# Batch 0 put in another order, and one load of batch 2 put later, in an attention and MLP kernel

## The chip, the core and the metric

The kernel runs on one core of one Trainium2 chip. The metric is the device time of one execution in microseconds (us): the median of several runs. A profiled execution also leaves a trace, with every instruction of the engines TensorE (PE for matmuls, PEld for the loads of their stationary operand), VectorE (DVE), ScalarE (ACT) and GpSimd (POOL), and the DMA transfers. SyncE (SP) only issues DMAs here.

## The reference, cut to what matters

Eight batches of eight heads; each head has 512 local and 32 global tokens of 64 numbers. Global queries attend to all keys; local queries attend to the global keys and to local keys at a distance of at most 32. The result, 4352 rows of 512 numbers, goes through an MLP with 2048 hidden units and the activation h * sigmoid(1.702 h).

```python
s_g = scale * np.matmul(q_g, k_all.transpose(0, 1, 3, 2))
out_g = np.matmul(sm(s_g), v_all)
s_ll = np.where(np.abs(pos[:, None] - pos[None, :]) <= window, s_ll, -1000000000.0)
a_l = sm(np.concatenate([s_lg, s_ll], axis=-1))
out_l = np.matmul(a_l, np.concatenate([v_g, v_l], axis=2))
...
h = x @ w_in
g = h * (1.0 / (1.0 + np.exp(-1.702 * h)))
return (g @ w_out)
```

## The kernel before

**Units of work.** Four heads of one batch make a quad; a batch has two, and the code calls the quad at hand `a` and the other `c`. Batch 0 is special: its quads are of class `Quad`, those of all other batches of class `Wide`. All work of a quad is a set of small methods, and the order in which the kernel calls them is the order on each engine: the schedule is written out by hand, and each engine works through its own instructions in that order.

**The methods of a `Quad`.** `Tk` and `Tq` transpose k and q on DVE (L306, L310); `ext` copies parts of the global queries beside them (L323 on ACT, L325 on DVE). `B(rnd)` writes the mask as a bias into the PSUM banks with a matmul against the identity (L335), `S(rnd)` adds the scores (L352), `X(rnd)` takes the exp on ACT (L380 for four single banks, L385 for two pairs). Each quad has two rounds, rnd 0 and 1, of two key chunks each. `gg` (through `gk`, L371) gives the scores of the global queries with the global keys, `K` those of the local queries with the global keys, and `XK` their exp (`ek`, L416). `ekU(unit)` and `U(unit)` sum weights (unit 0) and weighted values (units 1 and 2) into one bank per unit (L426, L438). `R` turns the sums into reciprocals in three DVE steps (L462, L464, L466), and `XL(h)` multiplies them in and gives one 128-row chunk of the MLP's input `xL` (L471): quad `a` gives chunks 0 and 1, quad `c` chunks 2 and 3. `eg` (DVE, L397), `Gm` (PE, L456) and `G` (DVE) make the outputs of the global queries. `zero(n, ...)` issues n filler matmuls of zeros (L646).

**PSUM.** `pbank` hands out four single banks in turn (tag "p"), for `ov`, `kb`, `og`, `hp` and `op`; `spair` gives the four others, as two pairs, for the scores and for the first four h tiles. A matmul into a bank waits until the bank's last reader is done. Within a quad of batch 0, round 1 uses the banks of round 0 again, except in quad `a`, whose round 1 has four single banks (`split=True`).

**The MLP.** `h_mm(i, fc, bank, kcs)` multiplies the chunks kcs of xL with w_in into an h tile (L586); `h_act` is a tanh on ACT (L593) and a multiplication on DVE (L594) that gives `gT`; `o_mm` multiplies with w_out (L611) and `o_out` scales and stores. The first four h tiles of batch 0 take chunks 0 and 1 first, then 2 and 3, and share their tanh in pairs (`tanh2`, L722; `act4`, L637). While the output matmuls of batch i run, the scores of batch i + 1 are put between them (`osteps` for batch 0, `phase_o` for the rest); in the h tiles of batch 1, `a.S(0)` of batch 2 follows h tile 10.

**Loads.** All loads of q, k, v and the weights cast from float32 to bfloat16 and are issued by POOL (`load`, L81; `load_v2`, L241; w_in, L254; w_out, L244), in the order of the program, among POOL's own computation: the affine select that makes `step` (L152), from which DVE makes `ident`, `band` and `bias` (L195 to L197), then constants and masks. A POOL load waits until the one eight places before it has landed. Only k of batch 0's first quad and the global rows of batch 0 come in float32 over ACT and SP, and ACT casts that k in two halves (`cast_k`, L649). w_in comes in four parts: the first two hold chunks 0 and 1, then 2 and 3, for the first eight h tiles.

```python
    warm = consts.tile([128, 512], BF16)
...
    for _ in range(7):
        nc.tensor.matmul(wp, lhsT=warm[:, :128], rhs=warm, start=True, stop=True)
```

Of the kernel before, what the change touches and what calls it, by code (L numbers as in the profile page):

```python
# [12 lines left out]
F32 = mybir.dt.float32  # L13
# [7 lines left out]
def kernel(  # L21
# [12 lines left out]
    nc = tc.nc  # L34
# [10 lines left out]
    NQ = B * 2  # L45
# [11 lines left out]
    consts = ctx.enter_context(tc.tile_pool(name="consts", bufs=1))  # L57
# [16 lines left out]
    def load(b, us=(0, 1), names="qk"):  # L74
        if b not in loaded:
            loaded[b] = (ld.tile([128, 2, 16 * D], BF16, name="rk"),
                         ld.tile([128, 2, 16 * D], BF16, name="rq"))
        s = slice(us[0], us[-1] + 1)
        for name in names:
            dst, src = ((loaded[b][0], kf), (loaded[b][1], qf))[name == "q"]  # L80
            nc.gpsimd.dma_start(out=dst[:, s], in_=src[b][:, s])  # L81
# [52 lines left out]
    def cast_g32(name, t):  # L134
        nc.vector.tensor_copy(t[:, 0:2, :D], g32[name])
# [5 lines left out]
    halves = (slice(0, 8 * D), slice(8 * D, 16 * D))  # L141
    load_g32("q", qgf)
    for f, eng in zip(halves, (nc.scalar, nc.sync)):
# [5 lines left out]
    nc.vector.memset(warm, 0.0)  # L149
    step = consts.tile([128, 289], BF16)  # L150
    nc.vector.memset(step, 1.0)
    nc.gpsimd.affine_select(  # L152
        out=step, in_=step, pattern=[[1, 289]], compare_op=ALU.is_ge,
        fill=0.0, base=-97, channel_multiplier=-1,
# [26 lines left out]
    for i in range(4):  # L181
        qt = consts.tile([128, 24, 32], F32, name="q%d" % i)
        nc.vector.memset(qt[:, 0:4, :], 0.0)
        nc.vector.memset(qt[:, 20:24, :], 0.0)
        qtiles.append(qt)

    WIN = ((0, 10), (6, 12), (14, 12), (22, 10))
    mask = consts.tile([128, 2, MW], BF16)
# [33 lines left out]
        nc.gpsimd.memset(mask_at(0, 248, 16, 12)[96:128, :, 0:4], 0.0)  # L222
        nc.gpsimd.memset(mask_at(1, 236, 16, 12)[96:128, :, 8:12], 0.0)

    load(0, (1,), "kq")
    load_turned(nc.gpsimd, rvg[:, 0:2, :D], vgf[:, 0:2])

    qgT = consts.tile([128, NQ, 40], F32)
    nc.vector.memset(qgT[:, :, 32:], 0.0)
    kgT = consts.tile([128, NQ, 32], F32)  # L230
    def transpose_g(lo, hi, names="qk"):
        for name, dst, s in (("q", qgT, rqg), ("k", kgT, rkg)):
# [15 lines left out]
    def load_rest():  # L248
        load_v2(0)
        set_consts()  # L250
        half = d_ff // 2
        for part in range(2):
            for u in range(2):
                nc.gpsimd.dma_start(out=w_in_sb[:, part, 2 * u : 2 * u + 2, :],  # L254
                                    in_=w_in_r[u][:, :, part * half : (part + 1) * half])
        load_w_out(1)
        load_w_out(0)
        mask_rest()
        for part in MASKS:
            make_mask(part)  # L260
        load(1, (0,))
        load_g(2, 4)
        load(1, (1,))
        load_vg(1)
        load_w_out(2)
        load_w_out(3)
        load(2, (0,))
        load_v(1)
        load_g(4, 8)

# [10 lines left out]
    def bank(pair, j):  # L281
        return pair[j // 2][:, j % 2, :]
# [301 lines left out]
    def h_mm(i, fc, hp, kcs):  # L584
        for kc in kcs:
            nc.tensor.matmul(hp[:, : width(i)], lhsT=w_in_c[:, fc // 8, kc, fc % 8 // 2, :, fc % 2],  # L586
                             rhs=(xL[i] if i < B else xG)[:, kc, :],
                             start=(kc == 0), stop=(kc == NKC - 1))
# [53 lines left out]
    a, c = Quad(0), Quad(1)  # L642

    def zero(n, ps, m=128, w=512):
        for _ in range(n):
            nc.tensor.matmul(ps[:m, :w], lhsT=warm[:, :m], rhs=warm[:, :w], start=False, stop=False, skip_group_check=True)  # L646

    def cast_k(f):
        nc.scalar.activation(rk[:, 0, f], k32[:, f], AF.Copy)  # L649

    cast_k(halves[0])
    cast_g32("q", rqg)
    transpose_g(0, 2, "q")
    a.ext((0, 1), True)
    cast_k(halves[1])
    a.Tk(0, 8)
    a.Tq(0, 8)
    a.Tk(8, 16)
# [4 lines left out]
    load_rest()  # L663
    a.B(0)
    a.B(1, split=True)
    zero(34, a.bk[1][3], 32, 32)
    a.S(0, added=True, part=0)
    a.S(0, added=True, part=1)
    a.X(0)
    a.S(1, split=True, added=True)  # L670
    zero(3, a.bk[1][3])
    a.X(1)
    c.Tk()
    c.ext()
# [5 lines left out]
    c.gg()  # L680
    c.X(0)
    a.eg()
    a.ekU(0)
    a.U(0)
    a.R()
    c.K()
    c.XK()
    a.ekU(1)
    a.U(1)
    a.XL(0)  # L690
    c.B(1, js=(0, 1))
    c.B(1, js=(2, 3))
    c.S(1, added=True)
    c.X(1)
    a.ekU(2)
    a.U(2)
    a.XL(1)
    a.Gm()
    gTs[0] = moe.tile([128, FC, TB], BF16, name="gT")
    pt = pts[0] = spair()  # L700
    c.ekU(0)
# [3 lines left out]
    c.U(1)  # L705
    c.ekU(2)
    c.U(2)
    c.eg()
    for fc in range(4):
        h_mm(0, fc, bank(pt, fc), (0, 1))  # L710
    c.XL(0)
    c.XL(1)
    for kc in (2, 3):
        for fc in range(4):
            h_mm(0, fc, bank(pt, fc), (kc,))
# [21 lines left out]
    nq = {b: (Wide(2 * b), Wide(2 * b + 1)) for b in (1, 2)}  # L737
    a, c = nq[1]
# [11 lines left out]
    a.S(1)  # L750
    a.X(1)
    spread_vg(1)
    nq[2][0].Tq()
    a.M(1)
    nq[2][0].Tk()
    osteps(0, (1, 2), (2, 2))
# [17 lines left out]
    a.G()  # L774
    transpose_g(4, 6)
    nq[2][0].ext(nc.gpsimd)
    load(2, (1,))
    load_v(2)
    load(3)
    osteps(0, (3, 2), (3, 3))  # L780
    a, c = nq[2]
# [4 lines left out]
    for fc in range(FC):  # L786
        if fc < 2:
            h_act(1, fc, hps[fc])
        else:
            h_step(1, fc)  # L790
        if fc == 1:
            nq[1][1].G()
        if fc == 10:
            a.S(0)
            a.X(0)
            a.M(0, nc.gpsimd)
            load_v(3)
            load(4)
            load_g(8, NQ)
# [101 lines left out]
```

## Time and profile before

| What | Value |
|---|---|
| Time, median of 3 runs | 299.2 us (299.19 to 299.46) |
| Time of the profiled execution | 299.52 us |
| Its span in the trace | 297.7 us |
| PE busy with matmuls | 291.9 us, 98% |
| VectorE, ScalarE, GpSimd busy | 219.1, 165.0, 79.7 us |
| First matmul, first matmul of the MLP | 1.26 us, 18.00 us |
| TensorE clock granted over the span | 1.00 |

The span reaches from the first to the last instruction of the trace; the time has 1.82 us more around it. All starts below are counted from the start of the span. In a row of the timeline come start and busy time, engine, line, operation, output and inputs with their shapes and the count of merged instructions; in brackets stands how long the engine had been idle before, and what ended that. Ends of matmuls are modelled: the distance between two starts tells more than their durations.

### The profile page before, as it was taken

What the parts mean: (1) busy time and instruction counts of PE and PEld (TensorE: products, weight loads), DVE (VectorE), ACT (ScalarE), POOL (GpSimd) and SP (SyncE); (2) the same over time, 40 slices, a digit from 0 to 9 for tenths busy, and PEclk for the clock granted to TensorE, in tenths of its full rate; (3) what the DMA queues carried; (4) which work ended last, traced back from release to release, by engine and by line L of the source; (5) the groups of instructions that cost most, each with busy time, mean ns of one, the idle gap of its engine ahead of it and who ended that gap; (6) DMA issues with size and microseconds to landing.
All of it is one profiled execution on the core that took longest, in us unless ns stands there. A gap on an engine that the chain in (4) does not pass through costs nothing.

```text
span 297.7 us, 8197 instructions
## 1 busy us (share of the span) xinstructions
PE 291.9 (98%) x3444; PEld 149.5 (50%) x3444; DVE 219.1 (74%) x440; ACT 165.0 (55%) x251; POOL 79.7 (27%) x130
## 2 busy tenths in 40 slices
PE   8999999999999999999999999999999999999995
PEld 5544446445454455445454455445554455446654
DVE  6669988869867887788878887778877866683320
ACT  3827375585557745567456655666446651663421
POOL 8962730589563002700072003500000000000000
PEclk9999999999999999999999999999999999999999
DMA  7999997699999213981299014901120022101122
GB/s 157 168 206 211 204 186 105 120 142 153 167 197 184 47 37 66 140 134 29 47 99 192 12 41 84 112 0 39 36 70 4 2 46 65 35 2 35 35 64 79
DMA packets 58228, 27.93 MB, mean 94 GB/s; under 512 B 47312, under 2 KB 47824, under 8 KB 58192
## 3 DMA queue, kind: packets, MB, share of 16 engines
q0 software_dynamic: 50784, 17.83, 53.2%
q1 hardware_dynamic: 7264, 9.31, 12.2%
q8 instruction: 27, 0.44, 0.6%
q10 hardware_dynamic: 144, 0.26, 0.3%
q14 instruction: 9, 0.07, 0.1%
HBM read 36.31 MB, written 8.91 MB: 152 GB/s over the span
## 4 chain that ended last, share of the span: by engine, by line
PE 96%; ACT 1%; DVE 1%; issue 0%
PE op L611 39%; PE hp L586 38%; PE s L531 6%; PE ov L557 5%; PE op L623 1%; PE w L178 1%; PE s L335 1%; PE og L568 1%; PE ov L438 1%; PE s L586 1%; ACT e L380 1%; ACT e L385 1%; DVE xL L471 0%; PE ov L426 0%; PE s L352 0%; PE s L557 0%
## 5 line engine op out<-in xcount | busy, mean ns | idle before, releaser
L611 PE MATMUL op<-w_out_sb,gT 128*128 128x512 bf16 x528 | 121.7, 379 | 0.0
L594 DVE SCALAR_TENSOR_TENSOR gT<-th,hp 128x512 bf16<-128x512 f32 (+1 forms) x140 | 91.2, 657 | 40.6 <-ACT th L593 39.7
L586 PE MATMUL hp<-xL,w_in_sb 128*128 128x512 bf16 x496 | 108.7, 379 | 0.0
L593 ACT ACTIVATE th<-hp 128x512 f32<-128x512 f32 (+1 forms) x140 | 79.8, 573 | 42.8 <-PE hp L586 40.9
L586 PEld LDWEIGHTS <-w_in_sb 128*128 128x128 bf16 x576 | 56.0, 98 | 64.9 <-DMA w_in_sb<-in_moe_w_in_dram 0.8
L611 PEld LDWEIGHTS <-gT 128*128 128x128 bf16 x528 | 49.3, 98 | 54.9
L542 ACT ACTIVATE e<-s 128x1016 bf16<-128x1016 f32 (+1 forms) x56 | 53.3, 1004 | 7.4 <-PE s L531 7.1
L626 ACT ACTIVATE ob<-op 128x512 f32<-128x512 f32 x32 | 18.9, 599 | 62.9 <-PE op L611 62.9
L97 POOL DMA_DIRECT2D v<-in_v_l_dram x35 | 28.4, 815 | 83.5 <-PE og L568 81.9
L547 DVE TENSOR_TENSOR e<-e,mask 128x1712 bf16<-128x1712 bf16 (+1 forms) x27 | 28.3, 1049 | 3.3 <-ACT e L542 3.3
L462 DVE STREAM_TRANSPOSE sT<-ov 128x512 f32<-128x512 f32 x15 | 10.7, 716 | 14.7 <-PE ov L557 12.6
L471 DVE TENSOR_TENSOR xL<-ov,rs 128x512 bf16<-128x512 f32 x30 | 19.4, 686 | 1.9 <-PE ov L438 0.5
L531 PE MATMUL s<-q,kT 32*128 32x160 bf16 (+3 forms) x672 | 19.2, 243 | 0.0
L531 PEld LDWEIGHTS <-kT 32*128 32x128 bf16 x672 | 13.1, 94 | 12.0 <-issue 6.5
L505 DVE STREAM_TRANSPOSE kT<-rk 128x512 f32<-128x512 f32 x14 | 14.5, 1033 | 0.0
L99 POOL DMA_DIRECT2D v<-in_v_g_dram x24 | 14.3, 595 | 0.0
L310 DVE STREAM_TRANSPOSE q<-rq 128x512 f32<-128x512 f32 (+1 forms) x17 | 11.5, 675 | 0.9 <-DMA rq<-in_q_l_dram 0.9
L466 DVE STREAM_TRANSPOSE rs<-rT 128x512 f32<-128x512 f32 x16 | 11.4, 711 | 0.6
L557 PE MATMUL ov<-e,v 128*32 128x128 bf16 (+3 forms) x624 | 11.7, 223 | 0.0
L557 PEld LDWEIGHTS <-v 128*32 128x32 bf16 x672 | 10.5, 97 | 0.0
L586 PE MATMUL hp<-xG,w_in_sb 128*128 128x256 bf16 x64 | 9.6, 273 | 0.0
L557 PE MATMUL ov<-e,ones 128*32 128x128 bf16 (+3 forms) x312 | 7.1, 225 | 0.0
(102 smaller groups left out, 156.3 us busy)
## 6 DMA issues: line engine op xcount, KB each, us to landing
out_dram<-ob SPq DMA_DIRECT2D x128, 64.0 KB, 1.7
v<-in_v_l_dram POOLq DMA_DIRECT2D x28, 96.0 KB, 4.4
rq<-in_q_l_dram POOLq DMA_DIRECT2D x5, 512.0 KB, 7.2
rk<-in_k_l_dram POOLq DMA_DIRECT2D x5, 512.0 KB, 9.3
w_in_sb<-in_moe_w_in_dram POOLq DMA_DIRECT2D x4, 512.0 KB, 10.5
w_out_sb<-in_moe_w_out_dram POOLq DMA_DIRECT2D x4, 512.0 KB, 12.0
v<-in_v_l_dram POOLq DMA_DIRECT2D x11, 128.0 KB, 4.7
rk<-in_k_l_dram POOLq DMA_DIRECT2D x5, 256.0 KB, 9.9
```

The lines of the kernel that those rows point to most:

```text
L97: nc.gpsimd.dma_start(out=vt[0:n, :, c, :D], in_=vs[FIRST[c] : FIRST[c] + n])
L471: nc.vector.tensor_mul(self.x[:, 2 * self.u + h, :], self.st[1 + h], self.st["rs"])
L505: nc.vector.transpose(flat[:, 0:Sl].rearrange("p (r t) -> p t r", t=16), loaded[self.b][0][:, self.u].bitcast(F32))
L531: nc.tensor.matmul(bank(self.ps, j)[:, at : at + n], lhsT=self.k[p, KEYS[c] : KEYS[c] + 128, e], rhs=self.q[p, lo:hi, r0 : r0 + nr, e], st ...
L542: nc.scalar.activation(self.E[rnd][:, 2 * i : 2 * i + 2, :n], self.ps[i][:, :, :n], AF.Exp, scale=scale)
L547: eng.tensor_mul(e, e, mask[:, rnd : rnd + 1, :n].to_broadcast([128, 4, n]))
L557: nc.tensor.matmul(ov[32 * j : 32 * j + 32, :].rearrange("p (t r) -> p t r", t=16)[:, t0:t1, r0 : r0 + nr], lhsT=lv, rhs=self.E[rnd][:, j, ...
L586: nc.tensor.matmul(hp[:, : width(i)], lhsT=w_in_c[:, fc // 8, kc, fc % 8 // 2, :, fc % 2], rhs=(xL[i] if i < B else xG)[:, kc, :], start=( ...
L593: nc.scalar.activation(th[:, :n], hp[:, :n], AF.Tanh, scale=0.851)
L594: nc.vector.scalar_tensor_tensor(gTs[i][:, fc, :n], in0=th[:, :n], scalar=1.0, in1=hp[:, :n], op0=ALU.add, op1=ALU.mult)
L611: nc.tensor.matmul(op, lhsT=gTs[i][:, fc, tci * 128 : tci * 128 + 128], rhs=w_out_sb[:, fc, :], start=(first and fc == 4 * f4), stop=(fc = ...
L626: nc.scalar.activation(ob, op, AF.Copy, scale=0.5)
```

## The change

The diff has seven parts. (1) The load of k of batch 0's second quad is issued by POOL ahead of the affine select instead of behind it; its q stays behind. The memset of `qgT` goes ahead of `ident` on DVE. (2) `cast_k` of the second half goes ahead of the first `ext` on ACT. (3) The 34 small fillers become 6 ahead of the first part of `a.S(0)`, 14 between its two parts, and 14 behind the three large fillers. (4) `c.K` goes ahead of `a.ekU(0)`, and `c.B(1)`, `c.S(1)` and `c.X(1)` go ahead of `a.U(1)` and `a.XL(0)`, with the two halves of `c.B(1)` around `a.ekU(1)`. (5) `a.Gm` goes behind the first eight matmuls of the MLP. (6) `c.eg` goes behind `c.XL(1)`. (7) q of batch 2's first quad is loaded ahead of batch 1's h tiles, with the second quad's q and k, instead of in `load_rest`; its `Tq` moves from the masks of batch 1 to behind h tile 6 of batch 1. No instruction that computes is added or taken away; the fillers stay 37 in all.

```diff
@@ -149,6 +149,7 @@
     nc.vector.memset(warm, 0.0)
     step = consts.tile([128, 289], BF16)
     nc.vector.memset(step, 1.0)
+    load(0, (1,), "k")
     nc.gpsimd.affine_select(
         out=step, in_=step, pattern=[[1, 289]], compare_op=ALU.is_ge,
         fill=0.0, base=-97, channel_multiplier=-1,
@@ -184,6 +185,9 @@
         nc.vector.memset(qt[:, 20:24, :], 0.0)
         qtiles.append(qt)

+    qgT = consts.tile([128, NQ, 40], F32)
+    nc.vector.memset(qgT[:, :, 32:], 0.0)
+
     WIN = ((0, 10), (6, 12), (14, 12), (22, 10))
     mask = consts.tile([128, 2, MW], BF16)

@@ -222,11 +226,9 @@
         nc.gpsimd.memset(mask_at(0, 248, 16, 12)[96:128, :, 0:4], 0.0)
         nc.gpsimd.memset(mask_at(1, 236, 16, 12)[96:128, :, 8:12], 0.0)

-    load(0, (1,), "kq")
+    load(0, (1,), "q")
     load_turned(nc.gpsimd, rvg[:, 0:2, :D], vgf[:, 0:2])

-    qgT = consts.tile([128, NQ, 40], F32)
-    nc.vector.memset(qgT[:, :, 32:], 0.0)
     kgT = consts.tile([128, NQ, 32], F32)
     def transpose_g(lo, hi, names="qk"):
         for name, dst, s in (("q", qgT, rqg), ("k", kgT, rkg)):
@@ -264,7 +266,7 @@
         load_vg(1)
         load_w_out(2)
         load_w_out(3)
-        load(2, (0,))
+        load(2, (0,), "k")
         load_v(1)
         load_g(4, 8)

@@ -649,10 +651,10 @@
         nc.scalar.activation(rk[:, 0, f], k32[:, f], AF.Copy)

     cast_k(halves[0])
+    cast_k(halves[1])
     cast_g32("q", rqg)
     transpose_g(0, 2, "q")
     a.ext((0, 1), True)
-    cast_k(halves[1])
     a.Tk(0, 8)
     a.Tq(0, 8)
     a.Tk(8, 16)
@@ -663,12 +665,14 @@
     load_rest()
     a.B(0)
     a.B(1, split=True)
-    zero(34, a.bk[1][3], 32, 32)
+    zero(6, a.bk[1][3], 32, 32)
     a.S(0, added=True, part=0)
+    zero(14, a.bk[1][3], 32, 32)
     a.S(0, added=True, part=1)
     a.X(0)
     a.S(1, split=True, added=True)
     zero(3, a.bk[1][3])
+    zero(14, a.bk[1][3], 32, 32)
     a.X(1)
     c.Tk()
     c.ext()
@@ -680,22 +684,21 @@
     c.gg()
     c.X(0)
     a.eg()
+    c.K()
     a.ekU(0)
     a.U(0)
     a.R()
-    c.K()
     c.XK()
+    c.B(1, js=(0, 1))
     a.ekU(1)
-    a.U(1)
-    a.XL(0)
-    c.B(1, js=(0, 1))
     c.B(1, js=(2, 3))
     c.S(1, added=True)
     c.X(1)
+    a.U(1)
+    a.XL(0)
     a.ekU(2)
     a.U(2)
     a.XL(1)
-    a.Gm()
     gTs[0] = moe.tile([128, FC, TB], BF16, name="gT")
     pt = pts[0] = spair()
     c.ekU(0)
@@ -705,11 +708,12 @@
     c.U(1)
     c.ekU(2)
     c.U(2)
-    c.eg()
     for fc in range(4):
         h_mm(0, fc, bank(pt, fc), (0, 1))
+    a.Gm()
     c.XL(0)
     c.XL(1)
+    c.eg()
     for kc in (2, 3):
         for fc in range(4):
             h_mm(0, fc, bank(pt, fc), (kc,))
@@ -750,7 +754,6 @@
     a.S(1)
     a.X(1)
     spread_vg(1)
-    nq[2][0].Tq()
     a.M(1)
     nq[2][0].Tk()
     osteps(0, (1, 2), (2, 2))
@@ -774,6 +777,7 @@
     a.G()
     transpose_g(4, 6)
     nq[2][0].ext(nc.gpsimd)
+    load(2, (0,), "q")
     load(2, (1,))
     load_v(2)
     load(3)
@@ -790,6 +794,8 @@
             h_step(1, fc)
         if fc == 1:
             nq[1][1].G()
+        if fc == 6:
+            a.Tq()
         if fc == 10:
             a.S(0)
             a.X(0)
```

## The prediction

> **What bounds the kernel now.** Times are microseconds from the span's start. I read the page, the chain of waits, the timeline by engine up to 70 us, then the DMA issues of short windows and the table of stretches. On the page TensorE (PE) is busy almost throughout:
>
> ```profile
> PE 291.9 (98%) x3444; PEld 149.5 (50%) x3444; DVE 219.1 (74%) x440; ACT 165.0 (55%) x251; POOL 79.7 (27%) x130
> ```
>
> The chain says when that begins. Ahead of 20.23 it runs over VectorE and ScalarE; behind it, over PE alone:
>
> ```profile
> 18.10 0.71 DVE rs L466
> 18.81 0.12 DVE eg L397
> 18.93 1.29 DVE xL L471 x2
> 20.21 0.02 issue
> 20.23 1.90 PE s L586 x8
> 22.13 0.27 PE og L456 x17
> 22.40 10.63 PE hp L586 x48
> 33.03 4.32 PE op L611 x20
> ```
>
> So the change is worth what it moves the matmul group at 20.23 (chunks 2 and 3 of the first h tiles), plus stalls behind it. The timeline shows two releasers of that group, hundredths apart:
>
> ```profile
> 18.00 1.90 PE L586 MATMUL s<-xL,w_in_sb 128*128 128x512 bf16 x8
> 20.22 1.41 PEld L586 LDWEIGHTS <-w_in_sb 128*128 128x128 bf16 x8 [0.82 <-DMA w_in_sb<-in_moe_w_in_dram]
> 20.23 1.90 PE L586 MATMUL s<-xL,w_in_sb 128*128 128x512 bf16 x8 [0.33 <-DVE xL L471]
> ```
>
> The weight load waits for the second w_in transfer, the matmul for xL. Both must come earlier for a gain. The DMA issues agree: the first w_in transfer, issued at 9.70, lands 7.8 later, at 17.5; the window with the first two has a median of 8.8, so the second (10.40) takes 9.8 and lands at 20.2.
>
> **The change part by part.** Deltas are made on the profiled execution, 299.52 (span 297.7 and 1.82 around it), and carried to the median, 299.2, which is 0.32 less.
>
> *k ahead of the mask.* One POOL issue (0.57, row L81) moves ahead of the affine select at 2.66 (0.46). step is ready at 3.65 instead of 3.12; ident, band and bias (3.15 to 3.93) end at 4.45; the qgT memset (0.17) fits the 0.51 that VectorE idles before ident. PE's first bias matmul goes from 4.23 to 4.5, 0.3 of idle. Eight bias matmuls then run 0.13 to 0.16 apart until 5.7, the other eight 0.07 to 0.08 apart as before, and end near 6.3 instead of 6.2. Nobody waits for that: the next scores need the second half of q, below. POOL's issues sum to the same, so w_in is still issued at 9.70.
>
> *Fillers and cast.* 34 fillers, 0.025 apart, took 0.86 at 6.26. Now 6 (0.15), 14 (0.35) and 14 (0.35). First-part scores start near 6.6 (k's transpose ends at 6.57) instead of 7.21. The second part still waits for VectorE's transpose of q's second half:
>
> ```profile
> 6.91 0.45 DVE L310 STREAM_TRANSPOSE q<-rq 128x256 f32<-128x256 f32 x1 [0.34 <-DMA rq<-in_q_l_dram]
> 7.92 1.66 ACT L385 ACTIVATE e<-s 128x856 bf16<-128x856 f32 x2 [2.19 <-PE s L352]
> ```
>
> So the first exp stays at 7.92 and the moved fillers cost nothing. The last 14 run from 9.13 to 9.48, where PE idles anyway (0.19, for ACT, until 9.63). Casting k's second half (0.61) before the ext copies delays the copies from 5.2 to 5.9; their reader starts at 6.6. Zero.
>
> *Second quad's scores.* ScalarE runs without a break from 7.92 to 13.91, then waits:
>
> ```profile
> 13.25 0.66 ACT L416 ACTIVATE ek<-kb 128x512 bf16<-128x512 f32 x1
> 14.98 1.66 ACT L385 ACTIVATE e<-s 128x856 bf16<-128x856 f32 x2 [1.07 <-PE s L352]
> ```
>
> c.K (0.43) goes into PE's 0.25 wait for ek before 11.83. The first half of the bias matmuls (0.36) starts at 12.57 behind a.U(0); the second half must wait until the exp of global scores ends (13.13 + 0.29), so the scores (0.6) start near 13.85, not 14.28, and the exp near 14.5, not 14.98. The chain behind it (c.U(0), three DVE steps of R, two xL of 0.65) moves by 0.45, and eg, put behind xL, frees 0.12 more: the last xL ends near 19.65 instead of 20.20. PE is ready for the first h matmuls at 17.55 instead of 18.00, just after their weights.
>
> *Global outputs.* a.Gm, 20 matmuls from 15.51 to 15.77 (0.26), moves into the hole before 20.23. PE's own work ends at 17.55 + 8 x 0.216 + 0.28 = 19.6. c.Gm's eg is ready near 19.8 and needed at 22.06. Zero.
>
> *What is late next: the weights,* at 20.2. The gain of all this is 20.23 - 20.20 = 0.03, with 0.5 of slack behind it, unless the transfers move. The table of stretches (last column GB/s) bounds that:
>
> ```profile
> 5.50:7.00 1.50, 1.50 (x39) 1.34 (x37) 1.02 (x3) 0.23 (x1) 1.50 (x3) 1.00 1.10 136
> 7.00:8.50 1.50, 1.50 (x68) 1.18 (x65) 1.12 (x5) 0.58 (x1) 1.50 (x2) 1.00 1.10 192
> 15.50:20.20 4.70, 4.40 (x100) 2.01 (x88) 3.77 (x8) 1.14 (x2) 3.66 (x9) 1.00 1.12 210
> ```
>
> If the low stretch is hunger for k's descriptors, an issue 0.45 earlier recovers (192 - 136) x 1.5 / 210 = 0.40. If the queue is full (DMA share 1.10 in both), nothing. k landed at 8.53 (3.03 + 5.5), 1.6 behind q's second half (6.9); the next transfer of its size took 1.45 (3.58 + 6.4 = 9.98). That neighbour is the nearest row: an excess of 0.15, of which I take 0.10. A loss is excluded: same bytes, same order, one queue. The Trainium skill (DMA: Bandwidth & Descriptors, Anatomy of one DMA) gives 2.0 us plus bytes / 436e3 for such a DMA, an estimate of 2.6 for k; the trace's 5.5 disagrees, and shows a queue. By that page k and all behind it would land with the issue, 0.45 earlier, and this term would be 0.4.
>
> *q of batch 2 later.* Out of the first stretch go one POOL issue (0.55 near 32.7), about 1.25 of transfer, and a VectorE transpose (0.71 at 42.04). The mask multiply behind it ends at 43.68; its reader, the U matmuls, starts at 46.46, so zero. Batch 1's last v load, issued at 38.37, lands near 46.9 and is read near 47.1: that cover of 0.2 grows by over 1, worth nothing today. Put back: an issue of 0.54 at 55.85, ahead of POOL's other loads and of its mask multiply at 65.73, which had 1.00 of idle before it. The transpose follows the seventh gT:
>
> ```profile
> 60.21 0.69 DVE L594 SCALAR_TENSOR_TENSOR gT<-th,hp 128x512 bf16<-128x512 f32 x1 [0.18 <-ACT th L593]
> 61.08 0.69 DVE L594 SCALAR_TENSOR_TENSOR gT<-th,hp 128x512 bf16<-128x512 f32 x1 [0.18 <-ACT th L593]
> ```
>
> The first load of that slot lands 4.5 after its issue, at 60.35, before VectorE comes (60.9). The next gT slips from 61.08 to 61.45; 0.17 of idle per step repays that in three steps. PE's eighth h bank is wanted again after the scores of 62.93, near 63.6, and is free at 62.2. Zero; landing after 62 it would cost its lateness.
>
> *A stall that the change doesn't name.* PE stood still in batch 1's second UG:
>
> ```profile
> 51.37 0.30 PE L568 MATMUL s<-v,e 96*32 96x66 bf16 x14 [0.38 <-issue]
> ```
>
> No releaser is known, and no later UG shows it. Gone, it is worth 0.4 to 0.6 (start to start); a second one costs as much. I take 0: the same instructions run there in both.
>
> Sum: -0.03 - 0.10, about -0.1: 299.4 for a profiled run, 299.1 for the median.
>
> **The rivals.** *Faster:* w_in lands early by the whole 0.40 (19.8); then xL (19.65) lets PE go near 19.8, -0.43, and the stall at 51.37 goes too, up to -0.57. Together 298.2 to 298.8; I take 298.5. For it: the 136 GB/s stretch, and lighter DMA before 51. Against: a DMA share over 1 throughout, and one cause would not give both.
>
> *Slower, the clock.* The bias matmuls of one size go from 0.16 apart to 0.08 apart at 5.7, 4.5 after PE's first matmul. The new idle of 0.3 at 4.23 lies inside that stretch. If the rise then comes only after the first scores, eight bias matmuls cost 0.6 more, the two score parts 0.25 each, fillers between them some 0.4, less the 0.5 of filler time saved: the first exp starts near 8.9 instead of 7.92, ScalarE's unbroken chain slips by 1.0, and 0.5 of slack is spent first. Decided at an exp start of 8.4; price 0.5 to 1.0, time 299.7 to 300.2, I take 300.0. Against: PE is still over 90% busy up to 5.7. The Trainium skill (TensorE: Matmul & The Clock Gate, The HAM clock gate) says the gate looks at a free-running window of about 3.4 us and opens after a busy one; that speaks for this rival as far as 0.3 idle spoils a window, and one more window from 5.7 would end at 9.1, an estimate from that page.
>
> *The move does nothing:* if the second half of the bias matmuls waits longer than 13.42, the exp stays at 14.98 and xL at 20.1. The time is the forecast's, since the weights hold PE anyway.
>
> **How the numbers follow.** About 0.2% (0.6) is what a measurement of this kernel can tell from no change. Forecast, with the move that does nothing: 0.45, own range 298.7 to 299.5. Faster rival: 0.35; its first half alone lies within 0.6, so it needs both halves or a recovery larger than I bounded. Slower: 0.20, the clock mostly. The range takes the faster rival's likeliest value less 0.1 and the slower one's lower part: 298.4 to 299.9.
>
> **What would show it.** Right: first exp at 7.92, the second quad's second exp near 14.5, its xL ending near 19.65, and the weight load of chunks 2 and 3 still ending its wait on w_in near 20.1. Faster rival: that load at 19.8, no gap near 51. Clock: bias matmuls still 0.16 apart after 5.8. Wrong altogether: PE idle over 0.2 between 22 and 33 or in h of batch 1, or the group of 20.23 starting after 20.3.

## The result and the profile after

| | Median of its runs | Ratio to before, 95% interval | Profiled execution (span) |
|---|---|---|---|
| kernel before | 299.20 us | | 299.52 (297.7) |
| changed kernel | 299.88 us | 1.0022, 1.0013 to 1.0031 | 300.85 (299.1) |
| changed kernel, second comparison (kernel before there: 299.14) | 299.42 us | 1.0013, 1.0004 to 1.0022 | 299.08 (297.3) |

The change makes the kernel slower, by 0.3 to 0.7 us. Two of the changed kernel's twenty executions, and two of twelve of order_early_k below, show a granted clock of 0.994 and take 1.1 to 1.6 more than the median; without them the changed kernel's median is 299.78, and order_early_k's 299.39. The first profiled execution is none of these, but still 1.0 above its median, so a second trace, from the run after_again, stands beside it below.

The page shows no more work, only a later and longer stretch for it:

```profile
PE 292.4 (98%) x3444; PEld 149.3 (50%) x3444; DVE 219.2 (73%) x440; ACT 165.2 (55%) x251; POOL 79.6 (27%) x130
```

Where the difference lies is read from starts of the same matmul groups in the two chains of waits. Kernel before (start, length, what):

```profile
53.50 9.50 PE hp L586 x44
...
87.43 13.81 PE hp L586 x64
...
290.88 3.51 PE op L623 x32
```

Changed kernel:

```profile
54.06 9.50 PE hp L588 x44
...
88.75 13.81 PE hp L588 x64
...
292.20 3.51 PE op L625 x32
```

From the first h tiles (22.40 before, 23.29 after) to the h tiles of batch 1 PE takes 31.10 before and 30.77 after; from there to batch 2, 33.93 and 34.69; from there to the end, 203.45 in both. So +0.89 comes from ahead of 22, -0.33 from the output stretch of batch 0, and +0.76 from batch 1. The last is one stall of PE, without a known releaser (0.77 from start to start), that no other trace of this study has:

```profile
74.97 0.52 PE L533 MATMUL s<-q,kT 32*128 32x228 bf16 x13 [0.51 <-issue]
```

The +0.89 is the change's own. The chain of the changed kernel up to the matmul group that was at 20.23 now begins with a load:

```profile
2.03 5.91 DMA rq<-in_q_l_dram
7.94 0.02 issue
7.96 0.46 DVE q L312
8.42 0.04 issue
8.46 0.48 PE s L354 x13
8.94 1.64 ACT e L387 x2
...
19.60 1.29 DVE xL L473 x2
20.89 0.13 DVE eg L399
21.03 0.09 DVE rg L478
21.11 1.90 PE s L588 x8
```

The timeline shows the same and the weights beside it (in brackets the idle time before, and what ended it):

```profile
6.93 0.42 PE L354 MATMUL s<-q,kT 32*128 32x120 bf16 x16 [0.39 <-DVE kT L308]
7.29 0.52 PE L648 MATMUL s<-warm 128*32 128x32 bf16 x14
7.96 0.45 DVE L312 STREAM_TRANSPOSE q<-rq 128x256 f32<-128x256 f32 x1 [1.08 <-DMA rq<-in_q_l_dram]
8.22 0.82 POOL L243 DMA_DIRECT2D v<-in_v_l_dram  x1 [0.40 <-DMA rq<-in_q_l_dram]
8.92 1.66 ACT L387 ACTIVATE e<-s 128x856 bf16<-128x856 f32 x2 [2.51 <-PE s L354]
10.14 2.91 POOL L256 DMA_DIRECT2D w_in_sb<-in_moe_w_in_dram  x4
...
15.61 1.66 ACT L387 ACTIVATE e<-s 128x856 bf16<-128x856 f32 x2 [0.66 <-PE s L354]
...
20.51 0.32 PE L458 MATMUL og<-v,e 128*32 128x66 bf16 x16
21.11 1.41 PEld L588 LDWEIGHTS <-w_in_sb 128*128 128x128 bf16 x8 [0.38 <-DMA w_in_sb<-in_moe_w_in_dram]
21.11 1.90 PE L588 MATMUL s<-xL,w_in_sb 128*128 128x512 bf16 x8 [0.25 <-DVE rg L478]
```

q's second half lands at 7.94 instead of 6.89; VectorE stands idle for it, and the first exp slips from 7.92 to 8.92. The same landing holds back POOL: the fourth v load waits for it, being eight loads behind, so w_in is issued at 10.14 instead of 9.70 and its second transfer lands at 21.06 instead of 20.18. In the row of 21.11 the matmul is put down to VectorE's rg, which ended just then but is no input of it: what it waited for is the weight load in the row above.

The low stretch of the DMA table rose only from 136 to 153 GB/s (last column), and the next one fell from 192 to 184:

```profile
5.50:7.00 1.50, 1.11 (x21) 0.88 (x22) 1.19 (x3) 0.92 (x3) 1.50 (x3) 1.00 1.09 153
7.00:8.50 1.50, 0.84 (x34) 0.72 (x38) 0.54 (x4) 0.00 (x0) 1.10 (x3) 1.00 1.09 184
```

Part 7 went as described. The transpose of q slips between two gT steps, and VectorE repays it:

```profile
61.37 0.70 DVE L312 STREAM_TRANSPOSE q<-rq 128x512 f32<-128x512 f32 x1
62.00 2.06 DVE L596 SCALAR_TENSOR_TENSOR gT<-th,hp 128x512 bf16<-128x512 f32 x3
```

### The profile page after: what moved, and what is told of

Its sections match the earlier page's. It is cut to its first block, busy times and chain, and to the rows that moved or that the text cites. A ratio compares the mean times of both kernels' runs of the same rounds, so it can differ in the third digit from the quotient of the medians.

```text
span 299.1 us, 8197 instructions
## 1 busy us (share of the span) xinstructions
PE 292.4 (98%) x3444; PEld 149.3 (50%) x3444; DVE 219.2 (73%) x440; ACT 165.2 (55%) x251; POOL 79.6 (27%) x130
## 3 DMA queue, kind: packets, MB, share of 16 engines
HBM read 36.31 MB, written 8.91 MB: 151 GB/s over the span
## 4 chain that ended last, share of the span: by engine, by line
PE 93%; DMA 2%; ACT 2%; DVE 1%; issue 1%; POOL 0%; DVEq 0%; POOLq 0%
PE op L613 39%; PE hp L588 38%; PE s L533 6%; PE ov L559 5%; DMA rq<-in_q_l_dram 2%; PE op L625 1%; ACT e L387 1%; PE og L570 1%; PE s L588 1%; ACT e L382 1%; DVE xL L473 0%; PE ov L440 0%; PE s L559 0%; PE s L354 0%; PE ov L428 0%
```

## The experiments

The first theory was A: k, put early into POOL's queue, delays the transfers around it. Its rival was B: landings differ from run to run and the place of k is nothing to them. Later ones are named where they came up. "The group" is the matmuls of chunks 2 and 3 of the first h tiles (20.23 in the kernel before). In the runs that put k back, the memset of `qgT` stays in its new place; k_alone and kq_first leave it in its old one. Where a matmul record is missing, the group's start is taken as the start of the first tanh of the h tiles (L722 of before) less 1.57, their distance in the kernel before.

### aa_before: the kernel before, unchanged

> The kernel before, unchanged, for a second trace and for the noise. Times within 0.3 us of the kernel before. Theory A (issuing k ahead delays the first transfers): q's second half lands at 6.9 us, the second w_in transfer at 20.2 us, as in the first trace. Theory B (the first transfers vary from run to run, whatever the order): these landings move by 0.5 us or more from the first trace.

Measured: 299.26, ratio 1.0007 (0.9997 to 1.0017). So 0.0007 can appear between a kernel and itself, within its interval. In its trace q's second half lands 0.40 later than in the first trace of this same kernel, the first exp starts at 8.27, and the group at 20.62: landings of one kernel scatter by about what the change does to them, and single traces prove little.

### k_alone: part 1 without the rest

```diff
+    load(0, (1,), "k")
     nc.gpsimd.affine_select(
...
-    load(0, (1,), "kq")
+    load(0, (1,), "q")
```

> The kernel before with one move alone: k of the second quad issued ahead of the affine select. Theory A: q's second half lands 0.5 to 1 us later than 6.9, the second w_in transfer near 21, and the time is 0.4 to 0.9 us over the kernel before. Theory B: no difference beyond 0.3 us; landings spread as in the unchanged kernel. The prediction's term for this move was -0.1 us.

Measured: 299.59, 1.0013 (1.0005 to 1.0022). First exp at 8.98, q's second half at 8.01, w_in issued at 10.20 and landed at 20.78, group at 20.83. This one part slows the kernel, as A had it.

### after_k_back: the change with k put back

```diff
-    load(0, (1,), "k")
     nc.gpsimd.affine_select(
...
-    load(0, (1,), "q")
+    load(0, (1,), "kq")
```

> The changed kernel with k of the second quad put back behind the affine select. Theory A: q's second half lands near 6.9 and w_in near 20.2 again, and the time is within 0.2 us of the kernel before, or up to 0.3 us under it. Theory B: it stays 0.4 to 0.9 us over the kernel before, as the changed kernel did.

Measured: 299.32, 1.0007 (0.9998 to 1.0016), as the unchanged kernel against itself. q's second half at 6.62, group at 19.96.

### after_again: the changed kernel once more

> The changed kernel, unchanged, for a second trace. 0.4 to 0.9 us over the kernel before. Theory A: q's second half lands near 7.9 again and the second w_in transfer near 21. Theory B: these landings differ from the first trace of this kernel by 0.5 us or more, and the loss comes from another place of the trace.

Measured: 299.42, 1.0013 (1.0004 to 1.0022); q's second half at 7.12, the earliest of any trace with k first. A is favoured by the two kernels with k first, but the traces overlap (7.12 against 7.29 in aa_before). And here it is not that landing that sets the first exp: it comes 1.28 behind it, at 8.41. The chain of waits runs from the issue of k over the late mask and slow bias matmuls:

```profile
2.58 0.53 POOL rk L81
...
4.52 2.45 PE s L337 x16
...
8.43 1.64 ACT e L387 x2
```

From the second on, the bias matmuls stayed 0.13 to 0.16 apart to the last; in the first trace of the change they were 0.08 apart from 5.5 on.

### mask_late and kq_first: half the edit, and twice the edit

With k first, the mask is also 0.5 later. mask_late has only that:

```diff
+    late = consts.tile([128, 448], BF16)
+    nc.gpsimd.memset(late, 0.0)
     nc.gpsimd.affine_select(
```

> The kernel before, with one POOL memset of 128x448 into a tile that nobody reads put ahead of the affine select (about 0.5 us, as long as the issue of k in the change); k stays behind. Theory A (k's transfer early in POOL's queue delays the transfers behind and beside it): nothing moves, q's second half lands at 6.6 to 7.3 and the second w_in transfer at 19.8 to 20.6, as in the three traces with k behind; time 299.0 to 299.4. Theory M (it is the mask that comes 0.5 later, not the queue): q's second half as before, but the first bias matmul at 4.5 to 4.7 and the first exp more than 1.1 behind that landing; time 299.4 to 299.8, as with k alone.

Measured: 299.78, 1.0021 (1.0012 to 1.0030). A's "nothing moves" is wrong. M has its signs (q's second half at 6.75, the first exp 1.46 behind it at 8.21) but not its reason: from that exp the group could start near 20.0, and yet it starts at 20.75. Its chain of waits runs through POOL alone:

```profile
2.58 0.44 POOL late L153
...
9.99 0.18 POOL v L171 x2
10.18 0.64 POOL w_in_sb L256
10.82 9.88 DMA w_in_sb<-in_moe_w_in_dram
20.70 0.05 issue
20.75 1.90 PE s L588 x8
```

Half a microsecond of work ahead on POOL pushes the issue of w_in from 9.70 to 10.12, and the landing goes with it (20.70). POOL's issue time is on the path, which the prediction had not seen.

kq_first puts both loads ahead:

```diff
+    load(0, (1,), "kq")
     nc.gpsimd.affine_select(
...
-    load(0, (1,), "kq")
```

> The kernel before, with both k and q of batch 0's second quad issued ahead of the affine select. Theory A: the suspected cost grows, q's second half lands later than 7.9, the second w_in transfer later than 20.8, time above 299.7. Theory B (landings differ from run to run and the place of k is nothing to them): q's second half anywhere from 6.6 to 8.0, time as with k alone, 299.4 to 299.7, what is lost being the mask that comes 1.1 late. Theory M: first bias matmul near 5.1, first exp set by PE and not by the landing, time 299.7 to 300.2.

Measured: 299.77, 1.0016 (1.0007 to 1.0025). q's second half at 7.62, first exp at 8.59 (0.97 behind it, so not set by PE and the mask), w_in landing at 20.27, group at 20.40. Slower, but the suspected cost did not double; A's numbers for it were too high.

### before_split and order_split: the weights taken off the path

```diff
-        for part in range(2):
+        for lo, n in ((0, half // 2), (half // 2, half // 2), (half, half)):
+            part, at = divmod(lo, half)
             for u in range(2):
-                nc.gpsimd.dma_start(out=w_in_sb[:, part, 2 * u : 2 * u + 2, :],
-                                    in_=w_in_r[u][:, :, part * half : (part + 1) * half])
+                nc.gpsimd.dma_start(out=w_in_sb[:, part, 2 * u : 2 * u + 2, at : at + n],
+                                    in_=w_in_r[u][:, :, lo : lo + n])
```

> The kernel before, with the first two w_in transfers (512 KB each, h tiles 0 to 7) cut in two: the columns of h tiles 0 to 3 for chunks 0, 1 and for chunks 2, 3 first, then those of h tiles 4 to 7. Theory W (the second w_in transfer ends the wait of the matmuls of 20.23 in the kernel before): the piece for chunks 2 and 3 of the first four tiles lands near 18.9, a quarter of 1 MB at 0.2 MB per us earlier; the matmuls then start at the end of xL, some 11.8 behind the first exp's start, 19.7 to 20.1, and the time is 298.7 to 299.0. Theory X (xL sets it in any case, as the chain of waits has it): group at 20.2 as before, 299.1 to 299.3.

Measured: 299.22, 1.0002 (0.9992 to 1.0011): no gain. The landing came early (16.56) and the group no longer waited for it: it started at 20.18, 11.81 behind the first exp, as W said (though not at the end of xL, which came at 20.64). But the first exp was at 8.37 in this trace, since PE was late; the chain of waits is PE alone from the mask on:

```profile
4.44 2.33 PE s L336 x16
6.77 0.94 PE s L647 x34
7.71 0.68 PE s L353 x30
8.39 1.64 ACT e L386 x2
```

The sixteen bias matmuls took 2.33, against 1.90 in the chain of before, where they go from 0.16 to 0.08 apart at 5.7; here they stay 0.13 to 0.16 apart to the end, as in after_again. So two chains of nearly one length meet at the group, and taking away one of them is worth little. The 7.92 of the first trace of before, on which the prediction stood, is an early value for that kernel.

order_split has, with this cut, the new order of the second quad and a.Gm in its old place:

> The changed kernel with k put back behind the mask, a.Gm put back to its place of before, and the w_in transfers cut as in the run before it. Theory W: with the weights out of the way the reordered second quad is worth its 0.4: chunk 2 and 3 matmuls start 11.5 behind the first exp's start, 19.4 to 19.7, and the time is 298.3 to 298.7, some 0.3 under the kernel before with the same cut. Theory X or a reorder that is worth nothing by itself: the same time as the kernel before with the cut, within 0.15.

Measured: 299.51, 1.0010 (0.9998 to 1.0021): the expected gain did not come. Two other loads were late in its trace:

```profile
11.04 3.51 POOL L256 DMA_DIRECT2D w_in_sb<-in_moe_w_in_dram  x5 [0.59 <-DMA rq<-in_q_l_dram]
11.54 0.66 PE L354 MATMUL s<-q,kT 32*128 32x200 bf16 x16 [0.41 <-DVE q L312]
21.36 1.04 PE L588 MATMUL s<-xL,w_in_sb 128*128 128x512 bf16 x4 [0.23 <-DMA w_in_sb<-in_moe_w_in_dram]
```

(Rows of POOL and of PE, in order of time.) The second quad's q landed at 10.76; its scores and their exp came 0.4 late, and POOL, which must see that landing before it issues a load eight places later, stood still for 0.59; so a further piece of w_in was late too, the fourth, and PE stood still until it landed (21.32), although it holds columns of h tiles 4 to 7. Why the matmuls wait for it is not shown. The cut adds issues to a queue that is itself on the path.

### w_in_early: the weights issued earlier, nothing else

```diff
         load_v2(0)
-        set_consts()
         half = d_ff // 2
...
                                     in_=w_in_r[u][:, :, part * half : (part + 1) * half])
+            if part == 0:
+                set_consts()
```

> The kernel before, with the first two w_in transfers issued ahead of the POOL constants (ones, bd and the ones in rvg and v), so at about 8.6 and 10.0 instead of 9.7 and 10.4. Theory P (the matmuls of 20.23 start at the later of two chains: the second w_in transfer's landing, which follows its issue, and 11.8 behind the first exp): the landing comes 0.3 to 0.8 earlier, 19.4 to 19.9, the group starts at the first exp plus 11.8, 19.7 to 20.2, and the time is 298.9 to 299.2, a gain of 0 to 0.3. Theory F (the DMA queue is full, and its order alone sets the landing): landing at 19.8 to 20.6 as in the traces of before, no gain, 299.1 to 299.4.

Measured: 299.04, 0.9988 (0.9980 to 0.9997). First w_in issue at 8.91, second landing at 19.72, group at 19.92, 11.81 behind the first exp (8.11): P's numbers. The second transfer's own issue moved less (10.26, against 10.40 and 11.07 in the two traces of before): POOL has to see the second quad's q land first (9.98 here). F is out: the queue's order did not change among the loads, only the time of issue, and the landing followed.

### order_alone and q2_alone: the other parts by themselves

order_alone is parts 2 to 6 (k, and q of batch 2, in their old places).

> Parts 2 to 6 of the change alone (fillers, cast, second quad, a.Gm, c.eg), with k behind the mask and q of batch 2 in its old place. Theory P: with a.Gm between the h matmuls PE reaches chunks 2 and 3 11.84 behind the first exp, as before (11.81), and the weights have not moved: 299.1 to 299.4, the same. Theory N (the new order is itself slower, since PE comes later to something that was hidden): above 299.5, with an idle stretch of PE or ScalarE between 8 and 22 that the kernel before has not.

Measured: 299.56, 1.0008 (0.9999 to 1.0016). Group at 20.21, right behind the weights (20.16), with the first exp at 7.86. No gain; a small loss is not excluded.

q2_alone is part 7.

> Part 7 alone: the kernel before with q of batch 2's first quad loaded later, and its transpose behind h tile 6 of batch 1. Theory P: nothing, 299.1 to 299.4; the h tiles of batch 1 start 33.5 apart from those of batch 2, as before. Theory Q (the later load or transpose is what costs): 299.5 to 299.8, with batch 1's 16 h tiles and scores longer by as much in the trace.

Measured: 299.37, 0.9997 (0.9989 to 1.0006): nothing, as the prediction had it. The two h phases are 33.49 apart, as before.

### order_early: both chains shorter

Parts 2, 3, 4 and 6 of the change, a.Gm and q of batch 2 in their old places, and the w_in of w_in_early.

> Parts 2 to 6 of the change, with a.Gm back in its place of before and the first two w_in transfers issued ahead of the POOL constants. Theory P: both chains are shorter, the landing at 19.4 to 19.9 and PE at the first exp plus 11.5; the group starts at 19.5 to 19.9 and the time is 298.6 to 298.9, faster than both kernels by 0.3 or more. Theory F: weights as before, 299.1 to 299.4.

Measured: 298.73, 0.9984 (0.9975 to 0.9993): faster than both kernels. w_in landed at 19.50, the group started at 19.74, 11.65 behind the first exp, with no stop between the h matmuls:

```profile
18.24 3.40 PE s L588 x15
21.64 0.28 PE og L458 x18
```

### order_early_again, order_early_k, order_early_gm, mask_late_early: the prices one by one

> Parts 2 to 4 and 6 of the change with the first two w_in transfers ahead of the POOL constants, once more, as the measure for the next two: 298.6 to 299.0, group of chunks 2 and 3 at 11.6 behind the first exp.

Measured: 298.96, 0.9991 (0.9981 to 1.0000). First exp at 8.33, group 11.60 behind it. The next two edits are made on this kernel; order_early_k:

```diff
+    load(0, (1,), "k")
     nc.gpsimd.affine_select(
...
-    load(0, (1,), "kq")
+    load(0, (1,), "q")
```

> The kernel of the run before it, with k ahead of the mask. Route 1 (over the first exp): first exp 0.4 to 0.8 later, near 8.7, the group 11.6 behind it near 20.3, and the time 0.3 to 0.6 above the kernel without it. Route 2 (over the issue of w_in alone): w_in issued within 0.2 of 9.0, landing near 19.6, and the time within 0.2 of the kernel without it.

Measured: 299.58, 1.0014 (1.0000 to 1.0029), 0.62 above the kernel without k first. w_in was issued at 9.34 and landed at 19.31, early; the group started at 20.41, 11.65 behind a first exp of 8.76. So with w_in early the cost of k is still there, and it goes over q and the first exp: route 1.

order_early_gm:

```diff
-    a.Gm()
     gTs[0] = moe.tile([128, FC, TB], BF16, name="gT")
...
         h_mm(0, fc, bank(pt, fc), (0, 1))
+    a.Gm()
```

> The kernel of the first run, with a.Gm behind the first eight h matmuls, as in the change. With the weights at 19.5 PE has no hole there: the 20 matmuls of 0.28 are on the path, group 11.84 behind the first exp, time 0.2 to 0.3 above the first run. As the prediction had it (a.Gm free in that place): the same time within 0.1.

Measured: 299.23, 1.0004 (0.9995 to 1.0013), 0.27 above the kernel with a.Gm in its old place, a difference that is itself uncertain by nearly as much. The chain shows the matmuls between the two halves:

```profile
18.50 1.83 PE s L588 x8
20.33 0.28 PE og L458 x17
20.61 1.83 PE s L588 x8
```

mask_late_early is the kernel of mask_late with the w_in of w_in_early:

> The kernel before with both the POOL memset of 0.5 ahead of the affine select and the first two w_in transfers ahead of the POOL constants. Over the issue of w_in: w_in at 9.3 and 10.0, landing 19.6 to 20.1, so the cost of the memset is gone: 299.0 to 299.3. Over the mask (bias matmuls and first exp late): as with the memset alone, 299.6 to 299.9.

Measured: 299.13, 0.9998 (0.9989 to 1.0007). The same memset that cost 0.6 costs nothing once w_in does not stand behind it (landing 19.87, group 19.93). For the memset the route is the issue of w_in; for k, in order_early_k, it is q's landing.

### order_early_fill and order_early_third: the small fillers

order_early_third is order_early once more; order_early_fill differs from it by this edit:

```diff
-    zero(6, a.bk[1][3], 32, 32)
+    zero(34, a.bk[1][3], 32, 32)
     a.S(0, added=True, part=0)
-    zero(14, a.bk[1][3], 32, 32)
     a.S(0, added=True, part=1)
...
-    zero(14, a.bk[1][3], 32, 32)
```

> Parts 2, 4 and 6 of the change with the first two w_in transfers ahead of the POOL constants, and the 34 small fillers ahead of the first score part, as before. If the 14 fillers between the parts are on the path when q's first half lands late: first exp at the later of that landing plus 1.8 and the second half's plus 1.0 (or set by a late clock, up to 8.4), the group 11.6 behind it, and the time 0.1 to 0.3 under the next kernel. If they are free, as the prediction had it: the same within 0.1.

> The kernel with the fillers in the new places, a third time, as the measure: 298.7 to 299.0; first exp no earlier than 2.28 behind the landing of q's first half.

Measured: 298.97, 0.9985 (0.9974 to 0.9996), and 298.90, 0.9992 (0.9978 to 1.0005): no difference in time. In both traces q's first half came early (5.65, 5.46) and the second half set the exp, 0.98 behind its landing, so this pair did not meet the case it was to price. That the fillers can be on the path is seen in order_early_again (first half at 6.05), whose chain runs from first part to fillers to second part:

```profile
7.06 0.43 PE s L354 x13
7.49 0.44 PE s L648 x14
7.94 0.41 PE s L354 x12
8.35 1.64 ACT e L387 x2
```

### What all twenty traces say together

The traces fit one rule within 0.05 (its three constants are taken from the same traces): the group starts at the second w_in landing plus 0.05, or at the first exp plus 11.81 (old order), 11.83 (new order) or 11.63 (new order, a.Gm in its old place), whichever is later. order_split is the one exception, with the late q told of above. "w_in issued" in the table is the first w_in transfer.

| Trace | q halves land | First exp | w_in issued, second landed | Group |
|---|---|---|---|---|
| before, aa_before | 5.62, 6.89; 6.11, 7.29 | 7.92; 8.27 | 9.70, 20.18; 9.71, 20.57 | 20.23; 20.62 |
| q2_alone | 5.61, 6.71 | 8.14 | 9.73, 20.04 | 20.13 |
| w_in_early | 6.19, 7.13 | 8.11 | 8.91, 19.72 | 19.92 |
| mask_late, mask_late_early | 5.59, 6.75; 5.50, 6.48 | 8.21; 7.47 | 10.12, 20.70; 8.93, 19.87 | 20.75; 19.93 |
| after_k_back, order_alone | 5.52, 6.62; 5.43, 6.88 | 8.13; 7.86 | 9.74, 19.77; 9.73, 20.16 | 19.96; 20.21 |
| order_early, order_early_again | 5.81, 6.89; 6.05, 6.83 | 8.09; 8.33 | 9.12, 19.50; 8.52, 18.91 | 19.74; 19.93 |
| order_early_gm | 6.42, 7.26 | 8.71 | 9.44, 19.81 | 20.54 |
| order_early_fill, order_early_third | 5.65, 6.99; 5.46, 7.02 | 7.97; 7.99 | 8.63, 19.37; 8.92, 19.56 | 19.58; 19.61 |
| before_split, order_split (w_in cut) | 5.47, 6.57; 5.61, 6.66 | 8.37; 8.05 | 9.76, 16.56; 9.74, 17.05 | 20.18; 20.11 |
| k first: k_alone | 7.18, 8.01 | 8.98 | 10.20, 20.78 | 20.83 |
| k first: changed kernel, twice | 5.92, 7.94; 5.84, 7.12 | 8.92; 8.41 | 10.14, 21.06; 9.71, 19.91 | 21.11; 20.24 |
| k first: kq_first | 5.83, 7.62 | 8.59 | 9.92, 20.27 | 20.40 |
| k first: order_early_k | 6.48, 7.78 | 8.76 | 9.34, 19.31 | 20.41 |

Over all twenty, the second half of q lands at 7.12 to 8.01 in the five traces with k first (mean 7.69), at 6.48 to 7.29 in the fifteen others (mean 6.86). Their first exps have means of 8.73 and 8.11. B is left with the scatter inside each set, some 0.4 to either side, but the difference between the sets, 0.8 and 0.6, is not scatter.

## Why the prediction was wrong, point by point

**The step that failed: "A loss is excluded: same bytes, same order, one queue."** From that the prediction took -0.10 for w_in, between 0 and -0.40. The runs show a loss: with k first, q's second half lands 0.8 later in the mean, although it was issued before k and at the same time as before. k itself, issued 0.45 earlier, lands at 8.55 to 9.39, mean 9.02, against a mean of 8.66 in the fifteen others. So an early issue helped nobody. What the part costs in time: 0.33 (k_alone against aa_before), 0.10 (after_again against after_k_back) and 0.62 (order_early_k against order_early_again), uncertain by 0.3, 0.2 and 0.5; weighted by that, about 0.2. k_alone is slower than the kernel before by itself (1.0005 to 1.0022), so the sign is shown. But 0.2 is a third to a half of what the change lost. The two kernels with the new order and k behind, after_k_back and order_alone, stand at 1.0007 and 1.0008, neither clear of the noise, so the rest stays open. That k's place delays q's landing is shown; how the transfers get into each other's way in the queue was not measured and stays open.

By the Trainium skill (DMA: Bandwidth & Descriptors, Anatomy of one DMA) each such transfer should end a fixed 2.0 plus its bytes / 436e3 behind its issue, and k should have come earlier with it. The 9.02 against 8.66 speaks against that for a queue with others in flight.

**The range.** 299.88 and 299.42 both lie inside 298.4 to 299.9. That is luck: the forecast's own mechanism gave 298.7 to 299.5 around a small gain, and the upper part was there for a late clock.

**"The first exp stays at 7.92"** fell too: 8.92, set by q's landing, and 8.41, set by PE and the late mask (below). The prediction saw that exp hang on q's second half and took that landing as given, with one trace for its evidence. The two traces of the kernel before differ by 0.40 in it.

**"w_in is still issued at 9.70."** The sum of POOL's issues was right, but the fourth v load has to see q's second half land. In three of the four traces with k first and the constants in their old place it was issued at 9.92, 10.14 and 10.20; in the two latest the bracket of a v load names a landing of q (0.40 and 0.47 of idle). The second w_in transfer waits in the same way for the second quad's q (0.30 of idle in k_alone). In addition the reading of a full queue was wrong in this sense: in the eighteen traces with w_in uncut, over issues from 8.5 to 10.2, the second landing came 10.0 to 10.9 behind the first w_in issue, so 0.4 on POOL is about 0.4 on the weights (mask_late, mask_late_early, w_in_early). This is the better use of the DMA share above 1: busy engines did not mean that issue time was free.

**"two releasers of that group, hundredths apart"** misreads the rows. The group's first four matmuls take chunk 2 alone, whose xL ended at 19.60; the 20.20 is the end of chunk 3, which only the next four need. The bracket names xL because that was the last event, and only the weights held the group. w_in_early shows it:

```profile
18.42 3.40 PE L587 MATMUL s<-xL,w_in_sb 128*128 128x512 bf16 x15 [0.16 <-issue]
19.10 1.29 DVE L472 TENSOR_TENSOR xL<-ov,rs 128x512 bf16<-128x512 f32 x2
```

There PE goes through its h matmuls without a stop and begins the group at 19.92, while xL runs until 20.39. So "Both must come earlier for a gain" was wrong: the second chain at the group is PE's own work, 11.81 behind the first exp, 19.73 in the trace of before. Earlier weights alone had up to 0.5 to gain there, and a last xL at 19.65 nothing.

**"The moved fillers cost nothing."** Not so whenever q's first half is late: the first exp is never less than 2.27 behind that landing in the new order, and as little as 1.81 in the old one, about the 0.45 of 14 fillers between the score parts. Seen in traces of other runs (order_early_again, order_early_gm, order_early_k); the run that was to price it in time did not. In the changed kernel's first trace the wait for the second half hid it. In its second, where PE is late, the new places are the cheaper ones: with slow bias matmuls to the end and the same start of 4.23, the first exp is at 8.37 with the fillers in their old place (before_split) and at 8.13 in the new ones (after_k_back).

**The second quad's scores.** Counted from the first exp, its second exp moved from 7.06 to 6.69 (after) and 6.64 (after_again): 0.37 to 0.42, predicted 0.48. The last xL moved from 12.28 to 11.97 and 11.93, so 0.31 to 0.35 where 0.55 was predicted; right in sign, 0.2 too large. It is not on the path, though, as said above.

**a.Gm "zero".** It lies in no hole: PE's own work reaches the group 11.83 behind the first exp with it and 11.63 without. The hole at 20.23 was there only as long as the weights were late. So the new order shortens PE's path by 0.2 and this move gives it back (0.27 in time in order_early_gm, uncertain by nearly as much). Together with late weights this is why parts 2 to 6 alone brought nothing (order_alone).

**What is late next.** "The weights, at 20.2" was right for that trace. With w_in early the prediction's faster rival works: 298.73. Its cause, an early k, was the wrong one, since k does not bring the weights.

**The slower rival** had the size, the threshold ("decided at an exp start of 8.4", 0.5 to 1.0) and, in one of two traces, the path. In the first trace of the change the bias matmuls were 0.08 apart long before the scores, and PE waited for q. In the second they never got there, and the first exp came at 8.41 with the mask 0.3 late on its path; after_k_back, as slow but without that 0.3, has 8.13. By that comparison the late mask cost 0.3 in this trace, which the prediction took as free ("Nobody waits for that"). What did not hold is the rival's cause, that the new idle of 0.3 makes the clock late. In kernels with k behind, the distance is halved anywhere from before 4.2 (order_early_gm) to after 6.4 (before_split, after_k_back); with k first from before 4.6 (k_alone) to after 6.6 (after_again). The granted clock of the stretches reads 1.00 here, before_split and after_again included, so the change is seen in the distances alone. The Trainium skill (TensorE: Matmul & The Clock Gate, The HAM clock gate) says that the gate's window is free-running, so that the same kernel meets it at another phase in each run; the scatter in the traces agrees, and gives no sign that the 0.3 of idle time decided.

**q of batch 2 and the stall at 51.37.** q's move cost nothing (0.9997). The stall was taken at 0, "the same instructions run there in both". The traces tie it to part 7 all the same: of the fifteen traces with q loaded early, twelve have a stall there, 0.3 to 0.6 from start to start; of the five with q loaded later, none has one of 0.3 or more. Three of these five have another one of 0.3 between 37 and 40, released by VectorE (q2_alone, after_k_back) or by a w_out transfer (order_split). So the price of the whole stretch barely moves: from the first tanh of batch 0 to the first of batch 1 it takes 32.82 in the mean with the later load, 32.90 with the earlier. The stall at 74.97 in the first trace of the change is in no other; its cause was not found.

Summed for the second trace, where no stall disturbs: the group at 20.24 against 20.23, so nothing gained or lost there; its 299.08 is 0.44 under the profiled kernel before because that trace's stall at 51 is missing. For the first: +0.88 at the group.

## What to carry to other kernels

Before an early load is called free, find everything that hangs on the landings around it: here one landing held VectorE, the first exp and, over the wait for the load eight places back, the issue of the weights. Where two chains of nearly one length meet, price each with the other removed, and take the starting point from several traces: a 7.92 that is 8.3 in the next run decides whether a term of 0.4 counts. On POOL, put the issue of what ends a chain ahead of constants that nobody needs yet: that alone gave 0.12% here, and 0.08 to 0.16% together with the new order, which these runs cannot tell apart, where the change itself lost 0.13 to 0.22%.

## What the runs showed of the hardware that was not expected

- A load issued 0.45 earlier (k, 256 KB) landed 0.36 later in the mean, not earlier, and one that was issued before it landed 0.8 later.
- With the DMA engines' share above 1 in the stretches before the landing (1.09 to 1.12 in the tables), the second w_in landing still followed POOL's issue, 10.0 to 10.9 behind it, for issues from 8.5 to 10.2.
- q's halves, the first loads of POOL, scatter by 1.0 and 0.8 between the fifteen traces with k behind, in which no load ahead of them differs, and the first exp with them.
- A VectorE copy of 128x192 that takes 0.26 took up to 0.73 when it began while POOL was issuing a v load (q2_alone, after_k_back, and shorter in others). In each of the nine traces where it took more than 0.28 it ended 0.06 to 0.09 behind the end of that issue; PE waited 0.3 for it at 37 in the two named. No run was made to test it.
